# Halved scores in the first half batch, and key pieces placed directly behind score pieces, in a sparse attention and feed-forward kernel

## The chip, the cores and the metric

The kernel runs on one core of one Trainium2 chip. Times are device microseconds (us) of that core for one execution, and a kernel is judged by the median of its runs. Faster and slower mean over 2% away from the kernel before (over 4.67 us here).

## The reference, cut to what matters

```python
# B=4 batches, H=8 heads, S=768 positions, D=64; 8 blocks of 96 positions per head
P = sort_net                                    # [4, 8, 8, 8], five rounds of normalisation
k_sorted = einsum('bhij,bhjcd->bhicd', P, k_b)  # mixes the 8 key blocks of a head
v_sorted = einsum('bhij,bhjcd->bhicd', P, v_b)
attn = softmax(q_block @ k_sorted_block.T / 8)  # within a block: 96 x 96
x = (attn @ v_sorted_block)                     # -> [3072 tokens, 512]
g = s * relu(x @ w_in) ** 2 + b                 # w_in 512 x 2048
out = g @ w_out                                 # w_out 2048 x 512
```

The two large products are nearly all of TensorE's work. Attention is many small matmuls that have to be put between them.

## The kernel before

The program order is written by hand. The 3072 tokens are eight tiles of 384 (two per batch, so tile 2 is the first half of batch 1). `ffn1` computes `hps` (x times w_in) with a "slot" after every pair of 128-row groups; `ffn2` computes `ops` (g times w_out) with a slot after every four matmuls. A queue of small pieces is dealt into the slots.

```python
psa = ctx.enter_context(tc.tile_pool(name="psa", bufs=3, space=PSUM))  # three double banks
psb = ctx.enter_context(tc.tile_pool(name="psb", bufs=2, space=PSUM))  # two single banks

def s_piece(t, hp):                 # scores of two heads: 8 matmuls, then Exp on ScalarE
    sc = psa.tile([BLK, 2, 512], FP, tag="a", name="sc")
    for n in range(HB):
        for e in range(2):
            nc.tensor.matmul(out=sc[:, e, n * BLK:(n + 1) * BLK], lhsT=ks[pr, g0 + n, :], ...)
    nc.scalar.activation(out=at, in_=sc[:, :, 0:TG], func=AF.Exp, scale=scale)

def p_piece(t, hp, n0=0, nn=HB):    # scores times V, then reciprocal and product on VectorE
    ...                             # pv in psb if nn < HB, else in psa
    nc.vector.reciprocal(out=rec[...], in_=pvv[:, :, :, D])
    nc.vector.tensor_tensor(out=x[...], in0=pvv[:, :, :, 0:D], in1=rec[...], op=ALU.mult)

def ffn1(t, slot=nothing, n0=0, nn=HB):
    for f0 in range(0, NF, 2):
        hps = psa.tile([128, 2, 512], FP, tag="a", name="hps")
        ...                         # 8 matmuls
        nc.scalar.activation(out=rt, in_=hps, func=AF.Relu)
        nc.vector.tensor_tensor(out=gt, in0=rt, in1=rt, op=ALU.mult)
        slot()
# k_piece (K): sorted keys "tk" in psa, four casts on VectorE ("v") or ScalarE ("s")
# v_piece1, v_piece2 (V1, V2): sorted values "tv" to DRAM; v_read brings them back as "vs"
# K(2, 32, 16, "s"): batch 2, positions 32 to 63 of each block, casts on ScalarE
# S2(3, 2), P2(3, 2): two s_piece, two p_piece (tile 3, head pairs 2 and 3).  T: x transposed by DMA.  q_turn: q transposed by DMA
gate2: nc.gpsimd.tensor_copy(out=gate2, in_=QT[2][...])   # the read of V waits for q's transpose
v_read(2, nc.gpsimd)
```

`hps`, `sc`, `tk`, `tv` of batches 1 to 3, and a full `pv`, all take turns on three double banks. A piece can start only when the piece three allocations earlier has been evicted.

The softmax here doesn't subtract the row's maximum and nothing guards it: scores larger than these inputs give would overflow.

## Time and profile before

| | before |
|---|---|
| time, median of 3 runs (us) | 233.47 (233.38 to 233.67) |
| span of the profiled run (us) | 231.6 |
| TensorE busy | 97% |
| VectorE, ScalarE busy | about half each |

The prediction shows the busy row, the clock row and the places it starts from. Two more views. The first is the list of what TensorE waited for, above 0.2 us in total (columns: total us, times, longest); it is short, and the first entry and the two cut out come before 17 us, at start-up.

```profile
PE wp L182 <- DVE warm L113: 1.1, 1, 1.1
...
PE ops L516 <- DVE ot L490: 0.4, 1, 0.4
PE hps L473 <- ACT rt L477: 0.3, 1, 0.3
```

The second is TensorE's timeline over the first slots of the first pass (start, duration, operation, count; a bracket gives idle time before it and what ended that). "hps 0" starts at 27.32, "hps 4" at 30.84; no line has a bracket, so nothing waits.

```profile
27.32 1.05 PE L473 MATMUL hps<-xt,wi 128*128 128x192 bf16 x8
28.20 0.30 PE L402 MATMUL pv<-vs,at 96*128 96x66 bf16 x4
28.34 0.83 PE L473 MATMUL hps<-xt,wi 128*128 128x192 bf16 x8
...
30.69 0.31 PE L402 MATMUL pv<-vs,at 96*128 96x66 bf16 x4
30.84 0.83 PE L473 MATMUL hps<-xt,wi 128*128 128x192 bf16 x8
```

### The profile page before, as it was taken

The page shows a single profiled execution, that of the slowest core. Times are in us where ns is not written, and L with a number is a line of the kernel's source. Part 1 is how long each engine was busy: PE and PEld are TensorE (multiplying, and loading weights), DVE is VectorE, ACT ScalarE, POOL GpSimd, SP SyncE. Part 2 cuts the span into 40 slices and gives each one's busy share as a digit, 9 for nine tenths or more (in the row PEclk, how much of TensorE's full clock was granted, in tenths as well). Part 3 has the DMA queues.
Part 4 walks back from the last instruction along what each step waited for, and adds up shares of the span by engine and source line. Part 5 has one row for each costly group of instructions (what it writes and reads, how often), then busy time and mean ns, then how long its engine had stood idle before and what let it go on. Part 6 is the DMA issues. An engine that isn't in the chain of part 4 may idle for free.

```text
span 231.6 us, 4837 instructions
## 1 busy us (share of the span) xinstructions
PE 224.3 (97%) x2036; PEld 136.8 (59%) x2036; DVE 116.8 (50%) x245; ACT 114.6 (49%) x164; POOL 48.3 (21%) x62
## 2 busy tenths in 40 slices
PE   8879999999999999999999999999999999999994
PEld 6779887765544555566555555665555556554442
DVE  5778566638992645244446653343452634432221
ACT  6168479685158486856630645656222236660000
POOL 7820000399992000007920000000000000000000
PEclk9975699999999999999999999999999999999999
DMA  5999999998799992764999995610115240001212
GB/s 93 142 200 211 226 193 205 231 220 183 106 110 180 273 312 63 161 82 65 130 148 133 183 197 115 93 47 0 46 47 113 93 110 4 3 0 45 80 59 91
DMA packets 46695, 28.90 MB, mean 125 GB/s; under 512 B 35921, under 2 KB 41041, under 8 KB 46161
## 3 DMA queue, kind: packets, MB, share of 16 engines
q0 software_dynamic: 18800, 15.21, 47.8%
q1 hardware_dynamic: 27728, 13.32, 26.6%
q8 instruction: 16, 0.26, 0.5%
q10 hardware_dynamic: 144, 0.07, 0.1%
q14 instruction: 7, 0.05, 0.1%
HBM read 29.63 MB, written 8.65 MB: 165 GB/s over the span
## 4 chain that ended last, share of the span: by engine, by line
PE 82%; DVE 7%; DMA 5%; ACT 3%; issue 1%; POOL 0%; POOLq 0%
PE hps L473 35%; PE ops L516 31%; DMA qr<-in_q_dram 5%; PE pv L402 4%; PE sc L375 3%; DVE gt L478 2%; ACT ks L240 2%; DVE ks L238 2%; PE tv L320 2%; PE ops L501 2%; PE tk L294 1%; PE tv L350 1%; PE wp L182 1%; PE tq L254 1%; PE tv L336 1%
## 5 line engine op out<-in xcount | busy, mean ns | idle before, releaser
L473 PE MATMUL hps<-xt,wi 128*128 128x384 bf16 (+1 forms) x576 | 87.1, 309 | 0.3 <-ACT rt L477 0.3
L516 PE MATMUL ops<-wo,gt 128*128 128x512 bf16 x368 | 86.9, 380 | 0.4 <-DVE ot L490 0.4
L473 PEld LDWEIGHTS <-wi 128*128 128x128 bf16 x576 | 54.1, 98 | 30.6 <-issue 1.3
L477 ACT ACTIVATE rt<-hps 128x768 bf16<-128x768 f32 (+1 forms) x72 | 53.1, 741 | 37.4 <-PE hps L473 37.0
L478 DVE TENSOR_TENSOR gt<-rt 128x768 bf16<-128x768 bf16 (+1 forms) x72 | 41.2, 574 | 50.2 <-ACT rt L477 50.0
L516 PEld LDWEIGHTS <-gt 128*128 128x128 bf16 x368 | 33.6, 98 | 37.2 <-issue 1.0
L378 ACT ACTIVATE at<-sc 96x768 bf16<-96x768 f32 x32 | 24.4, 804 | 27.7 <-PE sc L375 27.7
L490 DVE SCALAR_TENSOR_TENSOR ot<-ops,s_bc,bias 128x512 f32<-128x512 f32 x23 | 17.1, 749 | 41.2 <-PE ops L516 41.2
L240 ACT CAST ks<-tk 64x512 bf16<-64x512 f32 (+1 forms) x32 | 18.6, 582 | 10.5 <-PE tk L294 10.2
L407 DVE TENSOR_TENSOR x<-pv,rec 96x512 bf16<-96x512 f32 (+1 forms) x36 | 22.6, 627 | 1.3
L639 POOL TENSOR_TENSOR csum<-csum,wo 128x512 f32<-128x512 f32 x14 | 17.6, 1254 | 1.0
L402 PEld LDWEIGHTS <-at 96*128 96x128 bf16 (+1 forms) x256 | 12.0, 104 | 3.8
L182 PE MATMUL wp<-zt 128*128 128x256 bf16 x86 | 12.9, 311 | 1.1 <-DVE warm L113 1.1
L238 DVE CAST ks<-tk 64x512 bf16<-64x512 f32 (+1 forms) x20 | 13.0, 651 | 1.1 <-PE tk L294 0.8
L402 PE MATMUL pv<-vs,at 96*128 96x66 bf16 (+1 forms) x256 | 13.0, 199 | 0.1
L240 ACT CAST vn<-tv 128x512 bf16<-128x512 f32 (+1 forms) x12 | 9.4, 799 | 7.2 <-PE tv L350 5.0
L375 PEld LDWEIGHTS <-ks 64*96 64x96 bf16 x256 | 8.6, 128 | 5.8 <-issue 5.1
L406 DVE RECIPROCAL rec<-pv 96x8 f32<-96x8 f32 (+1 forms) x36 | 6.9, 192 | 9.5 <-PE pv L402 9.4
L84 POOL DMA_DIRECT2D qr<-in_q_dram x12 | 10.6, 912 | 4.8 <-DMA kb<-in_k_dram 3.1
L375 PE MATMUL sc<-qt,ks 64*96 64x96 bf16 x256 | 10.9, 219 | 0.1
L182 PEld LDWEIGHTS <-zt 128*128 128x128 bf16 x86 | 9.0, 110 | 2.6 <-DVE warm L113 1.1
L294 PEld LDWEIGHTS <-kb 64*128 64x128 bf16 x192 | 6.7, 99 | 3.9 <-issue 3.4
(73 smaller groups left out, 98.4 us busy)
## 6 DMA issues: line engine op xcount, KB each, us to landing
out_dram<-ot SPq DMA_DIRECT2D x23, 256.0 KB, 2.4
kb<-in_k_dram POOLq DMA_DIRECT2D x4, 768.0 KB, 12.2
vb<-in_v_dram POOLq DMA_DIRECT2D x4, 768.0 KB, 19.0
wi<-in_moe_w_in_dram POOLq DMA_DIRECT2D x2, 1024.0 KB, 19.7
wo<-in_moe_w_out_dram POOLq DMA_DIRECT2D x2, 1024.0 KB, 32.6
qr<-in_q_dram POOLq DMA_DIRECT2D x12, 128.0 KB, 13.5
dv<-vn SPq DMA_DIRECT2D x6, 256.0 KB, 7.5
vs<-dv POOLq DMA_DIRECT2D x4, 384.0 KB, 12.7
```

The lines of the kernel that those rows point to most:

```text
L182: nc.tensor.matmul(out=wp, lhsT=zt[:, 0:128], rhs=zt, start=True, stop=True)
L238: nc.vector.tensor_copy(out=out, in_=in_)
L240: nc.scalar.copy(out=out, in_=in_)
L375: nc.tensor.matmul(out=sc[:, e, n * BLK:(n + 1) * BLK], lhsT=ks[pr, g0 + n, :], rhs=QT[b][pr, hp, q0:q0 + BLK], start=True, stop=True)
L378: nc.scalar.activation(out=at, in_=sc[:, :, 0:TG], func=AF.Exp, scale=scale)
L402: nc.tensor.matmul(out=pv[e][0:m, (n - n0) * VW:(n - n0 + 1) * VW], lhsT=atf[:, c0:c0 + m], rhs=VS[b][:, gi, :], start=True, stop=True)
L407: nc.vector.tensor_tensor(out=x[:, n0:n0 + nn, hp * 128:(hp + 1) * 128].rearrange("p n (e d) -> p e n d", e=2), in0=pvv[:, :, :, 0:D], in1 ...
L473: nc.tensor.matmul(out=hps[:, f, 0:nt], lhsT=wi_at(hp, f0 + f), rhs=xt_at(t, hp, n0, nn), start=(hp == 0), stop=(hp == NHP - 1))
L477: nc.scalar.activation(out=rt[:, :, 0:nt], in_=hps[:, :, 0:nt], func=AF.Relu)
L478: nc.vector.tensor_tensor(out=gt[:, f0:f0 + 2, c0:c0 + nt], in0=rt[:, :, 0:nt], in1=rt[:, :, 0:nt], op=ALU.mult)
L516: nc.tensor.matmul(out=ops, lhsT=gt[:, f, m * 128:(m + 1) * 128], rhs=wo_at(f), start=(f == 0), stop=(f == NF - 1))
L639: nc.gpsimd.tensor_tensor(out=csum, in0=csum, in1=wo_at(f), op=ALU.add)
```

## The change

Its intent: in the head, only the half of tile 0's scores that is wanted at once is computed, and the other half is moved into slots of the first pass; one value piece and one score-times-V piece change places; and in batches 2 and 3 a key piece goes directly behind a score piece, so that the drain of TensorE between small and large matmuls is paid once for both.

```diff
+    def s_half(t, hp, n0, nn=2):          # as s_piece, for nn of the four blocks: 4 matmuls
+        sc = psa.tile([BLK, 2, 512], FP, tag="a", name="sc")
...
-    s_piece(0, 0) ... s_piece(0, 3)                    # head, among the value pieces
+    s_half(0, 0, 0) ... s_half(0, 3, 0)
+    def SH(hp):
+        return lambda: (s_half(0, hp, 2), s_half(0, hp + 1, 2))
-    ffn1(0, Queue([P(0, 0, 2, 2), P(0, 1, 2, 2), P(0, 2, 2, 2), P(0, 3, 2, 2),
+    ffn1(0, Queue([SH(0), SH(2), seq(P(0, 0, 2, 2), P(0, 1, 2, 2)),
+                   seq(P(0, 2, 2, 2), P(0, 3, 2, 2)),
                    lambda: q_half(1, "s"), lambda: t_piece(0, "v", 2, 2), SC(1, 0), SC(1, 1)], 8), 0, 2)
-    ... seq(SC(1, 3), P(1, 1)), V1(1), P(1, 2), P(1, 3),
+    ... seq(SC(1, 3), P(1, 1)), P(1, 2), V1(1), P(1, 3),
 # batch 2
-               V2[0], S2(2, 0), V2[1], S2(2, 2), V2[2], V2[3],
+               V2[0], V2[1], S2(2, 0), V2[2], S2(2, 2), V2[3],
-                  seq(T(2), K(2, 0, 16, "s")), P2(3, 0), S2(3, 2), K(2, 32, 16, "s"), P2(3, 2), T(3),
+                  T(2), P2(3, 0), seq(S2(3, 2), K(2, 0, 16, "s")), K(2, 32, 16, "v"), P2(3, 2), T(3),
 # batch 3
-                P2(4, 2), nothing, T(4), K(3, 0, 16, "v"), S2(5, 0), nothing, K(3, 32, 16, "s"),
-                P2(5, 0), nothing, S2(5, 2), nothing, P2(5, 2), K(3, 64, 16, "s"), T(5),
-                lambda: q_turn(3), nothing], 24)
+                P2(4, 2), nothing, T(4), seq(S2(5, 0), K(3, 0, 16, "v")), nothing, nothing, nothing,
+                P2(5, 0), seq(S2(5, 2), K(3, 32, 16, "s")), nothing, nothing, nothing, P2(5, 2),
+                T(5), K(3, 64, 16, "s"), lambda: q_turn(3)], 24)
```

K(2,32) also changes engine, from ScalarE ("s") to VectorE ("v").

More of the change, by code (lines that the diff above doesn't have):

```diff
@@ L379, in s_piece @@
         AT[t, hp] = at
+    def s_half(t, hp, n0, nn=2):
+        b, half = divmod(t, 2)
+        g0 = (b % 2) * 32 + hp * NB + half * HB
+        sc = psa.tile([BLK, 2, 512], FP, tag="a", name="sc")
+        for n in range(n0, n0 + nn):
+            for e in range(2):
+                pr = slice(e * 64, (e + 1) * 64)
+                q0 = (half * HB + n) * BLK
+                nc.tensor.matmul(out=sc[:, e, (n - n0) * BLK:(n - n0 + 1) * BLK],
+                                 lhsT=ks[pr, g0 + n, :], rhs=QT[b][pr, hp, q0:q0 + BLK],
+                                 start=True, stop=True)
+        at = atp.tile([BLK, 2, nn * BLK], BF, tag="at", name="ath")
+        nc.scalar.activation(out=at, in_=sc[:, :, 0:nn * BLK], func=AF.Exp, scale=scale)
+        AT[t, hp, n0] = at
     def p_piece(t, hp, n0=0, nn=HB):
         b, half = divmod(t, 2)
-        at = AT[t, hp]
+        halved = (t, hp, n0) in AT
+        at = AT[t, hp, n0] if halved else AT[t, hp]
         if t not in X:
@@ L398, in p_piece @@
             for n in range(n0, n0 + nn):
-                c0 = (e * HB + n) * BLK
-                m = 128 if c0 + 128 <= 2 * TG else BLK
+                c0 = (e * nn + n - n0) * BLK if halved else (e * HB + n) * BLK
+                m = 128 if c0 + 128 <= at.shape[1] * at.shape[2] else BLK
                 gi = e * 32 + hp * NB + half * HB + n
@@ L594 @@
     v_piece0(32, 16, "v")
-    s_piece(0, 0)
+    s_half(0, 0, 0)
     v_piece0(48, 8, "v")
-    s_piece(0, 1)
+    s_half(0, 1, 0)
     v_piece0(56, 8, "v")
-    s_piece(0, 2)
-    s_piece(0, 3)
+    s_half(0, 2, 0)
+    s_half(0, 3, 0)
     for hp in range(NHP):
@@ L619, in V1 @@
         return lambda: v_piece1(i * 8, eng)
-    ffn1(0, Queue([P(0, 0, 2, 2), P(0, 1, 2, 2), P(0, 2, 2, 2), P(0, 3, 2, 2),
+    def SH(hp):
+        return lambda: (s_half(0, hp, 2), s_half(0, hp + 1, 2))
+    ffn1(0, Queue([SH(0), SH(2), seq(P(0, 0, 2, 2), P(0, 1, 2, 2)),
+                   seq(P(0, 2, 2, 2), P(0, 3, 2, 2)),
                    lambda: q_half(1, "s"), lambda: t_piece(0, "v", 2, 2), SC(1, 0), SC(1, 1)], 8), 0, 2)
-    ffn1(0, Queue([seq(SC(1, 2), P(1, 0)), V1(0), seq(SC(1, 3), P(1, 1)), V1(1), P(1, 2), P(1, 3),
+    ffn1(0, Queue([seq(SC(1, 2), P(1, 0)), V1(0), seq(SC(1, 3), P(1, 1)), P(1, 2), V1(1), P(1, 3),
                    seq(V1(2), V1(3)), lambda: t_piece(1, "v")], 8), 2, 2)
@@ L652 @@
                + [lambda c0=c0: k_piece(1, c0, 16, 1, "vsv"[c0 // 32])() for c0 in range(0, BLK, 32)]
-               + [seq(lambda: load_q(2), lambda: load_k(*brows(2)), bias_piece), V2[0], S2(2, 0), V2[1], S2(2, 2), V2[2], V2[3],
+               + [seq(lambda: load_q(2), lambda: load_k(*brows(2)), bias_piece), V2[0], V2[1], S2(2, 0), V2[2], S2(2, 2), V2[3],
                   P2(2, 0), V2[4], P2(2, 2), V2[5], S2(3, 0),
-                  seq(T(2), K(2, 0, 16, "s")), P2(3, 0), S2(3, 2), K(2, 32, 16, "s"), P2(3, 2), T(3),
+                  T(2), P2(3, 0), seq(S2(3, 2), K(2, 0, 16, "s")), K(2, 32, 16, "v"), P2(3, 2), T(3),
                   seq(lambda: q_turn(2), K(2, 64, 16, "s"))], 24)
```

## The prediction

> **What bounds the kernel now.** I read the page first (busy table, slices, chain), then the chain in order of time, then the timeline of each engine around the four places that the diff touches.
>
> ```profile
> PE 224.3 (97%) x2036; PEld 136.8 (59%) x2036; DVE 116.8 (50%) x245; ACT 114.6 (49%) x164; POOL 48.3 (21%) x62
> PEclk9975699999999999999999999999999999999999
> PE 82%; DVE 7%; DMA 5%; ACT 3%; issue 1%; POOL 0%; POOLq 0%
> ```
>
> TensorE is the bound and hardly ever idle: only work taken off it, or stalls put on it, can move the 233.47 us. The clock row shows the one weak stretch, half clock from 14.1 to 27.8 us (the trace's clock record). The chain shows that VectorE ends the head:
>
> ```profile
> 22.97 0.70 DVE vs L238
> 23.67 0.04 issue
> 23.71 0.38 PE pv L402 x4
> ```
>
> and, from 53.8 to 70.3 us, holds TensorE once more: the bias, then an output eviction, frees a bank at 70.32. Elsewhere the matmuls set the pace. The timeline of TensorE's queue shows what a small piece costs between big matmuls:
>
> ```profile
> 125.90 0.52 PEld L294 LDWEIGHTS <-kb 64*128 64x128 bf16 x16 [0.42 <-issue]
> 127.44 0.43 PEld L375 LDWEIGHTS <-ks 64*96 64x96 bf16 x16 [0.42 <-issue]
> ```
>
> The weight load sits idle before each: it cannot run ahead. By single records, the last ops matmul before a key piece (tk) starts at 125.597 and the piece at 125.908, 0.311 us against the usual 0.216: 0.095 lost going in. The last tk starts at 126.355 and ops at 126.478, 0.123 against 0.029: 0.094 lost coming out. Score pieces (sc) lose 0.093 each way. A round trip costs 0.187 us.
>
> **What the Trainium skill says.** "TensorEngine Tiling (Array Packing)", Key Properties: "Mode switching requires drain". The trace agrees, with the 0.187 us. In the head, 64*96 scores and 64*128 value pieces follow each other without such a gap (score at 22.754 after 22.691, value at 22.666), so a key piece straight behind scores should save one round trip. "TensorE: Matmul & The Clock Gate", What's actually happening: the clock halves or doubles by windows of 3413 ns; the half-clock stretch here is 13.65 us, four such windows. "PSUM — Partial Sum Buffer", PSUM bank collisions: the chip does not arbitrate, so semaphores must keep a writer off a bank being read. The trace agrees: a matmul waits until the eviction of its bank ends (below).
>
> **Part 1, scores in halves.** In the head each score piece drops from 8 to 4 matmuls. At half clock a pair takes 0.09 us, so two pieces ahead of the last value piece free 0.36 us on TensorE. But VectorE still has its two evictions of 0.69 us in a row:
>
> ```profile
> 20.96 1.82 DVE L238 CAST vs<-tv 96x1024 bf16<-96x1024 f32 x2 [0.75 <-PE tv L320]
> 22.97 0.69 DVE L238 CAST vs<-tv 96x512 bf16<-96x512 f32 x1 [0.20 <-PE tv L320]
> ```
>
> The last can start at about 22.70, not 22.97: gain 0.27 us. Followed by half-clock work up to the window's end at 27.77, it is worth only 0.14 us at full clock.
>
> The other halves return in the first pass of hps slots, two pairs of pieces in slots 1 and 2, each with a round trip. There are three double banks for hps, sc and full pv. In the built program (buffers read from its listing) the new score tiles take two of the three, so hps 1 reuses the bank of hps 0 and hps 2 that of hps 1; before, each had its own. ScalarE now sits between:
>
> ```profile
> 28.40 0.49 ACT L477 ACTIVATE rt<-hps 128x384 bf16<-128x384 f32 x1 [1.53 <-PE hps L473]
> ```
>
> With 0.08 us per hps matmul and 0.246 us from last start to end: hps 0's last start 27.98, Relu 28.26 to 28.75; the halves are done by 28.46, so hps 1 waits to 28.79 (0.33). The same again at hps 2: 30.18 (0.33). The pv pieces then come two at a time, and VectorE's program has the third square ahead of them:
>
> ```profile
> 29.20 0.17 DVE L406 RECIPROCAL rec<-pv 96x4 f32<-96x4 f32 x1
> 29.41 0.42 DVE L407 TENSOR_TENSOR x<-pv,rec 96x256 bf16<-96x256 f32 x1
> ```
>
> hps 2's Relu ends 31.53, the square 31.90, the first pair of these 32.46, the second 33.11. The next two pv need exactly these two banks: they want to run at 31.77 and must wait to 32.50 and 33.15 (0.70 and 0.50). hps 4 starts at 33.29; before it started at 30.84. Loss 2.45 us, head gain included: 1.9 of waits, the rest two round trips (0.37) and 0.36 of scores, less the 0.14.
>
> **Part 2, V1 and P swapped.** In the second pass, one hps now waits for a Relu:
>
> ```profile
> 42.99 0.82 PE L473 MATMUL hps<-xt,wi 128*128 128x192 bf16 x8 [0.31 <-ACT rt L477]
> ```
>
> It was ready at 42.51, so 0.48 us is lost. In the new order its bank belongs to the pv two slots earlier, free in time; a new wait of about 0.2 comes for the earlier pv's eviction. Walked through: gain 0.28 us. Front in all: 2.45 - 0.28 = +2.2 us. The VectorE stretch from 54 to 70 starts from these matmuls and moves along.
>
> **Part 3, batch 2.** The order around the bank that comes free at 70.32 puts a value piece (0.43) before it and the score piece (0.49 + 0.093) behind: +0.16. One round trip is saved (-0.19), and so is a 0.14 us wait of S2(3,2) for a key eviction. But the merged key piece takes the bank of the second pv just one slot earlier:
>
> ```profile
> 85.38 0.20 DVE L406 RECIPROCAL rec<-pv 96x8 f32<-96x8 f32 x1 [3.28 <-PE pv L402]
> ...
> 86.52 0.69 DVE L407 TENSOR_TENSOR x<-pv,rec 96x512 bf16<-96x512 f32 x1
> ```
>
> That pv started at 84.91, the bank is free 2.30 us later; the key piece arrives after 0.54 + 0.864 + 0.093 + 0.40 = 1.90: wait 0.4. A pv further on waits 0.14 for the key's four casts (2.36 us on ScalarE). Walked from slot 18 to the first hps: 10.10 us against 9.88, with the 0.16: +0.38.
>
> And the moved key eviction, now on VectorE (four casts, 2.78 us as at 126.68), stands ahead of the last x of tile 3: x ends about 93.4, not 91.7 (+1.7). That feeds a serial queue: transpose of x, six transposes of q, the gate, then the read of V for batch 2.
>
> ```profile
> 91.74 1.28 SPq L452 DMA_TRANSPOSE xt<-x  x1
> 94.49 9.27 SPq L279 DMA_TRANSPOSE qt<-qr  x6
> 105.09 0.18 POOL L663 COPY gate<-qt 1x1 bf16<-1x1 bf16 x1 [34.34 <-DMA qt<-qr]
> ```
>
> That read lands at 116.69 (landing records); the pv that needs it starts at 117.24, so some 0.4 us of slack. 1.7 - 0.38 - 0.4 = a new wait of about 0.9 us there.
>
> **Part 4, batch 3.** Two merged pieces save 0.37. K(3,0) finds its bank free. K(3,32) does not: its pv stands right behind an output eviction on VectorE:
>
> ```profile
> 131.41 0.75 DVE L490 SCALAR_TENSOR_TENSOR ot<-ops,s_bc,bias 128x512 f32<-128x512 f32 x1 [1.95 <-PE ops L516]
> ...
> 133.14 0.69 DVE L407 TENSOR_TENSOR x<-pv,rec 96x512 bf16<-96x512 f32 x1
> ```
>
> The pv starts at 131.22, its second bank is free at 133.83 (+2.61), the key arrives at +1.9 and its scores are held 0.12 too: waits 0.77. Net +0.40.
>
> **Sum.** 2.2 + 0.4 + 0.9 + 0.4 = 3.9, so 233.47 + 3.9 = 237.4; I shade it to 237.0, because every wait is an upper figure when a neighbour is quicker than its row.
>
> **Rivals.** (a) The change does what it means to: fewer scores in the head and three round trips saved, 0.56 + 0.36 + some of the waits, 232.3 us. For it: TensorE is 97% busy and the drains are real. Against it: the bank map, which puts an eviction in front of each merged piece; VectorE, not scores, ends the head. (b) The waits come, but the read of V lands in time (fewer transfers in flight): 236.2. I can't see the transfers' contention. (c) The front's waits leave TensorE idle enough in one 3.41 us window for the clock to halve: up to 1.7 us more, 238.7. The window around 31.2 to 34.6 would be about two thirds busy; the window before 14.1 was some 60% busy with small tiles and fell. I give this 15%. (d) The head's earlier pv lifts the clock one window earlier (24.35, not 27.77): -1.7 us, 235.3. Against it: that window loses scores and gains only 0.27 us of dense work. 5%.
>
> **Range and chances.** The front's +2.2 has some 0.6 either way, the landing 0 to 1.2, batches 2 and 3 some 0.4 each: 235.0 to 238.7. 2% is 4.67 us, 238.14 or 228.80: slower by over 2% needs the clock to fall or every wait to be longer, 18%; faster by over 2% would need a gain four times what the drains can give, 1%.
>
> **What would show it.** Right: hps 4 of the first pass some 2.4 us later, idle before hps 1 and 2 put down to Relu and before the third and fourth pv to VectorE's x; key pieces behind scores with 0.4 and 0.7 us of wait for x and no idle weight load of their own; the first pv of tile 4 waiting for vs<-dv; hps of tile 2 half a microsecond later from the 70.3 anchor. Wrong: those waits absent, hps 4 at the old time, or a gap between scores and key pieces, which would mean the switch is not saved.

## The result, and the profile after

| | before | after |
|---|---|---|
| time, median (us) | 233.47 (233.34 to 233.67, 5 runs) | 237.76 (237.49 to 238.15, 5 runs) |
| ratio | | 1.0185 (95% interval 1.017 to 1.020): slower, but by less than 2% |
| span of the profiled run (us) | 231.6 | 236.3 |

Ratios here and below are the mean time of one kernel's fast runs over that of the other's fast runs of the same rounds, so they are not quite the ratio of the medians quoted. There is a difference: the stretch at half clock near the start lasts three or four of the clock's windows (10.24 or 13.65 us in the traces' clock records), and this varies between runs of one kernel. A run with three has a mean granted clock of 0.975 to 0.978, one with four 0.969 to 0.971. In one set of rounds six runs of the kernel before with three windows read 232.99 to 233.50 and five with four 233.33 to 233.87; their means differ by 0.4 us. Where a difference of that size matters, runs of equal clock are compared.

The page of the changed kernel, the lines that answer to those in the prediction. TensorE is about as busy in microseconds (224.2 against 224.3) in a longer span: the added time is idle time. (20 of its 2036 matmul records are missing from this trace, 2016 are there, so its busy time is up to some 0.8 us too low.) On the chain that ended last, VectorE's share has gone from 7% to 11% and TensorE's from 82% to 76%. The clock row is at 9 from the sixth slice (29.5 us) to the end.

```profile
PE 224.2 (95%) x2016; PEld 137.1 (58%) x2036; DVE 120.4 (51%) x249; ACT 112.4 (48%) x164; POOL 48.2 (20%) x62
PEclk9995699999999999999999999999999999999999
PE 76%; DVE 11%; DMA 4%; ACT 4%; issue 2%; POOL 0%; DVEq 0%
```

What TensorE waited for in the changed kernel. The first three shown are new, and the last has grown from one wait to two; each stands where a step of the prediction put it. Cut out are start-up and the head, a wait behind the bias that was there before (0.6, before 0.4), and 0.8 us put down to "issue", which are five gaps of 0.16 us where a matmul record is missing.

```profile
PE pv L419 <- DMA vs<-dv: 1.2, 1, 1.2
...
PE pv L419 <- DVE x L424: 0.9, 2, 0.6
PE tk L294 <- DVE x L424: 0.9, 2, 0.5
...
PE hps L490 <- ACT rt L494: 0.5, 2, 0.3
```

TensorE's timeline of the same first slots, changed kernel. Hps 1 and hps 2 wait for the Relu of the one before, and then two pv wait for VectorE's x, the product that empties their banks. Hps 4 starts at 33.39 where it started at 30.84.

```profile
27.36 0.94 PE L490 MATMUL hps<-xt,wi 128*128 128x192 bf16 x8
28.23 0.38 PE L390 MATMUL sc<-qt,ks 64*96 64x96 bf16 x8
28.88 0.82 PE L490 MATMUL hps<-xt,wi 128*128 128x192 bf16 x8 [0.27 <-ACT rt L494]
...
30.28 0.82 PE L490 MATMUL hps<-xt,wi 128*128 128x192 bf16 x8 [0.27 <-ACT rt L494]
...
32.62 0.31 PE L419 MATMUL pv<-vs,ath 96*128 96x66 bf16 x4 [0.58 <-DVE x L424]
33.25 0.30 PE L419 MATMUL pv<-vs,ath 96*128 96x66 bf16 x4 [0.32 <-DVE x L424]
33.39 0.83 PE L490 MATMUL hps<-xt,wi 128*128 128x192 bf16 x8
```

The bracket counts idle time after the modelled end of the matmul before, so it understates the delay. I therefore also compare the gap from the last start of one piece to the first start of the next, by single records, with the same gap where nothing waits. Hps 1 comes 0.475 us after scores instead of 0.138: a wait of 0.34, and the same at hps 2. The third pv comes 0.827 us after hps instead of 0.083: 0.74; the fourth 0.50 later than a pair would. Together 1.92 us.

The timelines further on, changed kernel: the merged key pieces and the first pv of tile 4. K(2,0) and K(3,32) wait for x, K(3,0) does not, and the pv waits for the read of V.

```profile
88.44 0.56 PE L375 MATMUL sc<-qt,ks 64*96 64x96 bf16 x16
89.39 0.62 PE L294 MATMUL tk<-pd,kb 64*128 64x64 bf16 x16 [0.40 <-DVE x L424]
...
121.59 0.58 PE L419 MATMUL pv<-vs,at 96*128 96x66 bf16 x13 [1.17 <-DMA vs<-dv]
...
130.65 0.63 PE L294 MATMUL tk<-pd,kb 64*128 64x64 bf16 x16
...
137.35 0.64 PE L294 MATMUL tk<-pd,kb 64*128 64x64 bf16 x16 [0.46 <-DVE x L424]
```

Start to start, K(3,0) follows its scores by 0.044 us, where a key piece behind large matmuls takes 0.311: the saved drain is real. K(2,0) takes 0.600, K(3,32) 0.665.

The way to the late read of V, in the timelines of VectorE, of SyncE's DMA queue and of GpSimd, changed kernel: the key casts run from 91.59, x of tile 3 ends at 96.18 (before: 91.68), its transpose starts at 96.25 (before: 91.74), and the gate is passed at 109.10 (before: 105.09).

```profile
91.59 2.79 DVE L238 CAST ks<-tk 64x512 bf16<-64x512 f32 x4 [1.69 <-PE tk L294]
...
95.49 0.69 DVE L424 TENSOR_TENSOR x<-pv,rec 96x512 bf16<-96x512 f32 x1
```

```profile
96.25 1.28 SPq L469 DMA_TRANSPOSE xt<-x  x1
...
99.00 8.82 SPq L279 DMA_TRANSPOSE qt<-qr  x6
```

```profile
109.10 0.18 POOL L684 COPY gate<-qt 1x1 bf16<-1x1 bf16 x1 [35.80 <-DMA qt<-qr]
```

The starts of six common points in the two profiled runs show where the 4.7 us of span came in:

| first start of | before | after | later by | so this stretch added |
|---|---|---|---|---|
| hps 4, first pass | 30.84 | 33.39 | 2.55 | 2.55 |
| hps of tile 1 | 47.08 | 49.59 | 2.51 | -0.04 |
| ops behind the bias | 70.32 | 72.87 | 2.55 | 0.04 |
| hps of tile 2 (batch 2's slots done) | 92.38 | 95.40 | 3.02 | 0.47 |
| first pv of tile 4 | 117.24 | 121.59 | 4.35 | 1.33 |
| hps of tile 4 (batch 3's slots done) | 140.47 | 145.19 | 4.73 | 0.37 |

### The profile page after: what moved, and what is told of

It is laid out like the page before. It is cut to its first block, busy times and chain, and to the rows that moved or that the text cites. A ratio compares the mean times of both kernels' runs of the same rounds, so it can differ in the third digit from the quotient of the medians.

```text
span 236.3 us, 4822 instructions
## 1 busy us (share of the span) xinstructions
PE 224.2 (95%) x2016; PEld 137.1 (58%) x2036; DVE 120.4 (51%) x249; ACT 112.4 (48%) x164; POOL 48.2 (20%) x62
## 4 chain that ended last, share of the span: by engine, by line
PE 76%; DVE 11%; DMA 4%; ACT 4%; issue 2%; POOL 0%; DVEq 0%
PE hps L490 30%; PE ops L533 29%; PE wp L182 6%; DMA vs<-dv 4%; PE pv L419 3%; DVE gt L495 3%; PE sc L375 2%; DVE x L424 2%; DVE ks L238 2%; ACT rt L494 2%; PE ops L518 1%; PE tk L294 1%; PE tv L320 1%; ACT ks L240 1%; DVE vs L238 1%
## 5 line engine op out<-in xcount | busy, mean ns | idle before, releaser
L533 PE MATMUL ops<-wo,gt 128*128 128x512 bf16 x349 | 83.1, 379 | 2.2 <-issue 0.8
L378 ACT ACTIVATE at<-sc 96x768 bf16<-96x768 f32 x28 | 21.3, 803 | 32.3 <-PE sc L375 32.3
L240 ACT CAST ks<-tk 64x512 bf16<-64x512 f32 (+1 forms) x28 | 16.3, 583 | 11.9 <-PE tk L294 11.6
L238 DVE CAST ks<-tk 64x512 bf16<-64x512 f32 (+1 forms) x24 | 15.9, 661 | 2.9 <-PE tk L294 2.6
L182 PE MATMUL wp<-zt 128*128 128x256 bf16 x86 | 14.2, 334 | 1.1 <-DVE warm L113 1.1
L419 PEld LDWEIGHTS <-at 96*128 96x128 bf16 x224 | 9.6, 102 | 4.4 <-issue 1.6
L182 PEld LDWEIGHTS <-zt 128*128 128x128 bf16 x86 | 9.8, 120 | 3.3 <-DVE warm L113 1.1
L419 PE MATMUL pv<-vs,at 96*128 96x66 bf16 x224 | 10.1, 195 | 1.2 <-DMA vs<-dv 1.2
L375 PEld LDWEIGHTS <-ks 64*96 64x96 bf16 x224 | 6.3, 121 | 5.8 <-issue 5.1
L375 PE MATMUL sc<-qt,ks 64*96 64x96 bf16 x224 | 8.4, 210 | 0.0
```

Source lines behind the costliest of these rows:

```text
L182: nc.tensor.matmul(out=wp, lhsT=zt[:, 0:128], rhs=zt, start=True, stop=True)
L238: nc.vector.tensor_copy(out=out, in_=in_)
L240: nc.scalar.copy(out=out, in_=in_)
L419: nc.tensor.matmul(out=pv[e][0:m, (n - n0) * VW:(n - n0 + 1) * VW], lhsT=atf[:, c0:c0 + m], rhs=VS[b][:, gi, :], start=True, stop=True)
L533: nc.tensor.matmul(out=ops, lhsT=gt[:, f, m * 128:(m + 1) * 128], rhs=wo_at(f), start=(f == 0), stop=(f == NF - 1))
```

## The experiments

The theory from here on is the prediction's own: most moves put a bank's next user too close behind its last one, so that evictions on ScalarE and VectorE, and one read of V behind them, set the pace. Its rivals: the added pieces cost their TensorE time as such, or the clock does it. Eleven kernels were run besides the two, all with correct results; they are labelled e1 to e11. "Before" in each paragraph is the kernel before in the same rounds.

**The halved scores alone.** (e1) The kernel before with the head and the first pass of the change, nothing else.

> The kernel before with the halved scores alone (head and the first four hps slots as in the change; nothing else). My account (waits for Relu and for the x evictions): 2.3 to 2.5 us slower, 235.9 us; the fifth hps group of the first pass starts 2.4 us later than before after the same start of the value pieces, with idle TensorE before hps 1 and 2 (0.27 each, Relu) and before the third and fourth pv (0.6 and 0.3, x). Rival, the loss is only the added work (two round trips 0.37 and 0.36 of scores, head gain off): 0.5 to 0.8 us slower, 234.1 us, and the rest of the 4.3 us lies in the key pieces.

```diff
-    s_piece(0, hp) in the head;  P(0, 0, 2, 2), P(0, 1, 2, 2), P(0, 2, 2, 2), P(0, 3, 2, 2)
+    s_half(0, hp, 0) in the head;  SH(0), SH(2), two P per slot
```

236.36 us (235.97 to 236.47, 4 runs) against 233.35; ratio 1.0125 (1.0111 to 1.0139), a loss of 3.0 us. All four runs had the fourth half-clock window, so hps 0 and the first halves ran at half clock; against runs of before with four windows the loss is about 2.6 us. In its profile hps 4 starts at 33.89, 3.05 us after its old place where 2.4 was expected; but its half clock lasted to 29.12 and that of before to 27.77, so runs with equally many windows are still not quite alike. The profile's list of waits has the two of the theory, with the sizes they have in the changed kernel:

```profile
PE pv L419 <- DVE x L424: 0.9, 2, 0.6
PE hps L490 <- ACT rt L494: 0.6, 2, 0.3
```

**The swap alone.** (e2) `V1(1), P(1, 2)` becomes `P(1, 2), V1(1)`.

> The kernel before with only the pv piece and the value piece of batch 1 swapped in the second pass. By the prediction 0.28 us faster (a 0.48 us wait for Relu replaced by 0.2 for an x eviction), 233.2 us. By the trace of the changed kernel, where the hps groups gained 0.16 and then waited 0.12 for the transposed x, nearly nothing: 0 to 0.1 us.

```diff
-    seq(SC(1, 3), P(1, 1)), V1(1), P(1, 2), P(1, 3),
+    seq(SC(1, 3), P(1, 1)), P(1, 2), V1(1), P(1, 3),
```

233.28 us (233.11 to 233.68) against 233.35; ratio 0.9997 (0.9985 to 1.001). In the times it is worth nothing that can be measured, not the predicted 0.28 us. The traces resolve a little: from hps 4 to hps of tile 1 it takes 16.20 us, against 16.24 before.

**The two queues of batches 2 and 3 alone.** (e3)

> The kernel before with only the two queues of batches 2 and 3 as in the change (key pieces moved, value pieces reordered). My account: 0.47 (batch 2) + 1.33 (the first pv of tile 4 waits for the read of V) + 0.37 (batch 3) = 2.2 us slower, 235.6 us, and with the halves alone the two sum to the whole 4.3 to 4.7. Rival, the late read of V comes from the front's delay and not from the key eviction: no such wait here, 0.8 us slower, 234.3 us.

```diff
 # the batch 2 and batch 3 parts of the change, on the kernel before
```

235.38 us (235.0 to 235.73) against 233.35; ratio 1.0085 (1.007 to 1.0101), 2.0 us. The wait for the read of V is there without the front's part, so it comes from the queue of batch 2:

```profile
PE pv L419 <- DMA vs<-dv: 1.0, 1, 1.0
```

The two parts run alone lose 2.6 us (at equal clock) and 2.0 us; their sum 4.6 is close to the change's 4.3 in the medians and 4.7 in the profiled runs.

**The second key piece evicted by ScalarE again.** (e4) The changed kernel, one letter different, so that the key casts are no longer ahead of x on VectorE.

> The changed kernel with one letter different: the second key piece of batch 2 is evicted by ScalarE instead of VectorE. My account: x of tile 3 ends 1.4 us earlier, so the transposes of q, the gate and the read of V start 1.4 us earlier, and the 1.33 us wait of the first pv of tile 4 goes: 1.2 to 1.4 us faster than the changed kernel, 236.4 us. Rival, the read is late because of other transfers beside it: wait and time as in the changed kernel, 237.7 us.

```diff
-    K(2, 32, 16, "v"), P2(3, 2), T(3),
+    K(2, 32, 16, "s"), P2(3, 2), T(3),
```

237.0 us (236.38 to 237.17, 4 runs); ratio to before 1.015 (1.0134 to 1.0167). At equal clock it is 1.1 to 1.4 us faster than the changed kernel, and the wait for `vs<-dv` is gone from the list. It is gone only just: by the landing records the read is complete at 119.83, and the pv starts at 119.97.

**The other order on VectorE.** (e9) A second test of the same chain, by another means: the casts stay on VectorE, but P2(3,2) and so the last x go first.

> The changed kernel with one exchange in batch 2: the scores-times-V piece P2(3,2) goes ahead of the second key piece K(2,32), whose eviction stays on VectorE. My theory: the V read of batch 2 is late because the four key casts stand ahead of the last x of tile 3 on VectorE. Then x of tile 3 ends some 2 us earlier, the wait of the first pv of tile 4 for vs<-dv (1.2 us) is gone, and the time falls by 1.1 to 1.4 us from the changed kernel: ratio to before 1.012 to 1.014. Rival (the read is late because ScalarE's or the matmuls' share moved, or because the transfers collide): the wait for vs<-dv stays at 0.8 us or more and the ratio stays at 1.017 to 1.020.

```diff
-    K(2, 32, 16, "v"), P2(3, 2), T(3),
+    P2(3, 2), K(2, 32, 16, "v"), T(3),
```

236.77 us (236.43 to 237.04, 4 runs) against 233.47; ratio 1.0141 (1.0122 to 1.0159), at the upper edge of what was expected and clear of the rival's 1.017. X of tile 3 is transposed from 93.60 instead of 96.25, the read is complete at 119.09, and the pv follows the matmuls before it without a bracket:

```profile
118.69 2.11 PE L533 MATMUL ops<-wo,gt 128*128 128x512 bf16 x9
120.63 0.70 PE L419 MATMUL pv<-vs,at 96*128 96x66 bf16 x16
```

From hps of tile 2 to this pv it takes 24.86 us, against 26.19 in the changed kernel: 1.33 us, the whole wait. Moving the eviction to the other engine and moving it behind x have the same effect, so the order of VectorE's queue is the cause.

**Batch 3's queue alone, and the same with one piece moved.** In the first (e5), batch 3 is as in the change. In the second (e6), P2(5,0) goes one slot earlier, so that its banks are free when K(3,32) arrives.

> The kernel before with only the queue of batch 3 as in the change. My account: two mode switches saved (0.37) and 0.77 of waits for x at the second merged key piece: 0.37 to 0.4 us slower from the first ops of that queue to the first hps after it (27.27 us before), total 0.2% slower. Rival, the merging saves what it means to: 0.37 us faster there.

> The same queue, but the pv pieces of the second half stand one slot earlier, so that two slots lie between them and the scores with the second key piece, and no output eviction stands before them on VectorE. My account: both waits go and the two saved switches stay: the queue takes 0.37 us less than in the kernel before, total 233.0 us. Rival, the drain is not saved by standing behind scores: no less than before.

```diff
-    seq(S2(5, 0), K(3, 0, 16, "v")), nothing, nothing, nothing, P2(5, 0), seq(S2(5, 2), K(3, 32, 16, "s")),
+    seq(S2(5, 0), K(3, 0, 16, "v")), nothing, nothing, P2(5, 0), nothing, seq(S2(5, 2), K(3, 32, 16, "s")),
```

As in the change: 233.69 us (233.49 to 234.23) against 233.56, ratio 1.0012 (0.9998 to 1.0026). From hps of tile 2 to that of tile 4 it takes 48.46 us against 48.08 before, +0.38, which the profile resolves and the times don't. With the piece moved: 232.81 us (232.70 to 233.37), ratio 0.9972 (0.9959 to 0.9985), the same stretch 47.66, -0.42. The timeline of K(3,32) in each, first as in the change, then moved:

```profile
131.67 0.72 PE L375 MATMUL sc<-qt,ks 64*96 64x96 bf16 x16
132.85 0.64 PE L294 MATMUL tk<-pd,kb 64*128 64x64 bf16 x16 [0.46 <-DVE x L424]
```

```profile
131.77 0.56 PE L375 MATMUL sc<-qt,ks 64*96 64x96 bf16 x16
132.17 0.63 PE L294 MATMUL tk<-pd,kb 64*128 64x64 bf16 x16
```

So a merged piece does save its drain (two save 0.42 us), and in the change the wait for a bank took more than it gave. One slot decides the sign.

**A first attempt at a better kernel.** (e7) The swap, batch 3 moved as above, and in batch 2 K(2,0) behind S2(3,0) with its eviction on VectorE. The load of K for batch 2 is also issued before that of q.

> A candidate to beat both: whole scores in the head, the swap of the second pass, the queue of batch 3 with the pv pieces one slot earlier, and in batch 2 the first key piece straight behind the scores of tile 3's first half (evicted by VectorE; K loaded before q so that it is there). Where three switches are saved and no bank is in use: 0.37 + 0.19 + 0.14 (a wait of scores for a key eviction) + 0.1 = 0.8 us faster than the kernel before, 232.6 us at equal clock. It fails to reach that if the earlier key eviction delays the x of the next pv, or the read of V.

```diff
-    seq(lambda: load_q(2), lambda: load_k(*brows(2)), bias_piece)
+    seq(lambda: load_k(*brows(2)), lambda: load_q(2), bias_piece)
-    V2[5], S2(3, 0), seq(T(2), K(2, 0, 16, "s")), P2(3, 0), S2(3, 2), K(2, 32, 16, "s"), ...
+    V2[5], seq(S2(3, 0), K(2, 0, 16, "v")), T(2), P2(3, 0), S2(3, 2), K(2, 32, 16, "s"), ...
```

233.63 us (232.97 to 234.0) against 233.56; ratio 0.9999 (0.9983 to 1.0014): a miss. Two things went against it. Five of its six runs had the fourth half-clock window, against seven of eleven of before; at equal clock it is 0.1 us faster with four windows, and 0.4 with three (one run). And in batch 2 the casts on VectorE delayed the x behind them, so the second half of S2(3,2) waited:

```profile
86.76 0.38 PE L375 MATMUL sc<-qt,ks 64*96 64x96 bf16 x8
87.51 0.38 PE L375 MATMUL sc<-qt,ks 64*96 64x96 bf16 x8 [0.37 <-DVE x L424]
```

From the ops behind the bias to hps of tile 2 it took 22.28 us against 22.06 before, +0.22. It is the same mistake as the change's: a key eviction on VectorE in front of an x.

**The same with the eviction left on ScalarE** (e10), without the swap.

> The kernel before with batch 3 of e6 (P2(5,0) one slot early) and, in batch 2, only the first key piece moved behind the score piece S2(3,0), its eviction left on ScalarE. If a merged piece is worth its saved round trip wherever its bank is free, this gains 0.19 us on e6: ratio 0.996 (0.9945 to 0.9975), 232.6 us at equal clock windows, with 0.04 us between the last score and the first key matmul in batch 2 and no wait for x above 0.2 us at S2(3,2). Rival: the earlier key eviction delays a later bank as in e7, S2(3,2) or P2(3,0) waits 0.3 us or more, and the ratio is 0.997 to 0.999, no better than e6.

```diff
-    V2[5], S2(3, 0), seq(T(2), K(2, 0, 16, "s")), P2(3, 0),
+    V2[5], seq(S2(3, 0), K(2, 0, 16, "s")), T(2), P2(3, 0),
```

232.67 us (232.43 to 232.93, 5 runs) against 233.47; ratio 0.997 (0.9957 to 0.9983). In the profile batch 2's stretch takes 21.87 us against 22.06, the 0.19 us of one drain. It does not come as I wrote: the key piece follows its scores by 0.20 us, not 0.04, so part of the saving is lost there. No bank causes this: the trace shows the key piece released by the read of K, which landed at 82.41 where the scores' last matmul started at 82.26. In e7, whose K was loaded first and landed at 75.97, the key piece followed its scores by 0.042. As much is won back where S2(3,2) no longer waits for a key eviction (gap 0.309 instead of 0.450 before). In the times it can't be told from the kernel with batch 3 alone (0.9972), whose rounds were others. It is faster than both kernels of this study, in the medians by 0.8 us against the kernel before (0.6 to 0.8 at equal clock): real, and far under 2%.

**The halves, one per slot.** (e8) If the four waits are most of the front's loss, the same halves spread out should cost little more than their drains.

> The halves alone as in e1_halves, but the returning halves come one to a slot and the pv pieces one to a slot, so that no bank is taken back within two slots and none of the waits for Relu and x should be left. Work stays, with two round trips more than in e1_halves. My account: the waits are 1.9 of the 2.4 us, so this is 0.9 to 1.2 us slower than the kernel before, 234.4 us, against some 3.0 of e1_halves. Rival, the loss is the added work: as slow as e1_halves or slower, as there are more switches.

```diff
-    ffn1(0, Queue([SH(0), SH(2), seq(P(0, 0, 2, 2), P(0, 1, 2, 2)), seq(P(0, 2, 2, 2), P(0, 3, 2, 2)),
-                   q_half, t_piece, SC(1, 0), SC(1, 1)], 8), 0, 2)
+    ffn1(0, Queue([HF(0), HF(1), seq(HF(2), P(0, 0, 2, 2)), seq(HF(3), P(0, 1, 2, 2)),
+                   seq(P(0, 2, 2, 2), q_half), P(0, 3, 2, 2), seq(t_piece, SC(1, 0)), SC(1, 1)], 8), 0, 2)
```

236.38 us (235.79 to 236.61) against 233.56; ratio 1.0113 (1.0098 to 1.0129): a miss. The four waits are gone, but my order made a fifth, seen in the timelines of TensorE, ScalarE and VectorE:

```profile
36.56 0.26 PE L447 MATMUL tr<-ident,x 96*128 96x96 bf16 x2 [1.11 <-DVE x L424]
```

```profile
33.67 1.50 ACT L240 COPY qt<-tq 128x768 bf16<-128x768 bf16 x2 [0.53 <-PE tq L254]
35.06 0.89 ACT L494 ACTIVATE rt<-hps 128x384 bf16<-128x384 f32 x2
```

```profile
35.60 0.36 DVE L495 TENSOR_TENSOR gt<-rt 128x384 bf16<-128x384 bf16 x1 [1.52 <-ACT rt L494]
35.88 0.17 DVE L423 RECIPROCAL rec<-pv 96x4 f32<-96x4 f32 x1
36.08 0.42 DVE L424 TENSOR_TENSOR x<-pv,rec 96x256 bf16<-96x256 f32 x1
```

Read it backwards: the transposes wait for the last x, x stands on VectorE behind a square (gt), the square waits for its Relu, and the Relu stands on ScalarE behind 1.50 us of q copies that I had put one slot too early. The transposes were held up by three queues in turn.

**The halves, one per slot, with q behind the last pv.** (e11)

> The kernel before with the halved scores, but the returned halves one per slot, each pv piece one per slot behind the next half, the query piece behind the last pv, so that no Relu, square or q cast stands in front of a bank wanted next (what I had missed in e8). Theory (four waits are most of the +2.5 us): hps 4 of the first pass comes 0.5 to 1.0 us after its old place (30.84), no wait above 0.3 us for Relu or x and none of 1 us at the transposes; time 233.47 + 0.4 to 0.9, ratio 1.002 to 1.005 at the same number of half-clock windows. Rival (halves cost their time as such, or the clock does it): ratio 1.009 or more again with no wait named.

```diff
+    ffn1(0, Queue([HF(0), seq(HF(1), P(0, 0, 2, 2)), seq(HF(2), P(0, 1, 2, 2)), seq(HF(3), P(0, 2, 2, 2)),
+                   P(0, 3, 2, 2), q_half, seq(t_piece, SC(1, 0)), SC(1, 1)], 8), 0, 2)
```

235.44 us (234.76 to 235.66, 6 runs) against 233.47; ratio 1.0086 (1.0071 to 1.01). The first half of the expectation holds, the second does not. Hps 4 starts at 31.74, 0.90 us after its old place, and no line before it has a bracket:

```profile
28.14 0.29 PE L390 MATMUL sc<-qt,ks 64*96 64x96 bf16 x4
28.36 0.83 PE L490 MATMUL hps<-xt,wi 128*128 128x192 bf16 x8
29.13 0.29 PE L390 MATMUL sc<-qt,ks 64*96 64x96 bf16 x4
29.35 0.31 PE L419 MATMUL pv<-vs,ath 96*128 96x66 bf16 x4
...
31.74 0.83 PE L490 MATMUL hps<-xt,wi 128*128 128x192 bf16 x8
```

That is about what four separate halves should cost: four drains of 0.187 and 0.36 us of scores are 1.1 us, against 1.04 measured from hps 0 to hps 4 beyond before, where this order has one pv piece less (the fourth comes behind hps 4). By the first hps of tile 1 it is 1.45 us later than before (48.53 against 47.08). The 0.55 us more are that pv piece and two waits of 0.24 and 0.20 us at later hps: one for the q copies on ScalarE, and one for the copy of the transposed x, which stands on VectorE behind a square whose Relu stands behind the q copies. The time is 2.0 us worse in the medians, 1.5 to 1.8 at equal clock. The ratio lies where the rival put it, at 1.009, but with waits that can be named. For the change this means: 1.9 of its front's 2.5 us are the four waits, which another order does without, but that order paid for two more drains and for waits further on. I found no order in which the halves pay.

## Why the prediction was right

237.0 us was predicted and 237.76 measured, inside the range and on the right side of zero, and the mechanism was right in its main parts: new waits for evicted banks and for a read, nearly all put down by the profile to the engines that the prediction had named. Two terms were mis-sized: the swap, and the wait for the read of V. The sizes, step by step:

- **Halved scores, +2.45.** Measured +2.55 at hps 4. The four waits, 0.33, 0.33, 0.70 and 0.50, came as 0.34, 0.34, 0.74 and 0.50. The halves alone give nearly the same waits, the spread order (e11) has none of them and hps 4 moves to +0.90. The two profiled runs differ in clock (half clock to 27.77 before, to 27.29 after) and in when the value pieces start (17.95 and 18.15), which nearly cancels: from that start to hps 4, five three-window traces with the old front (e2, e3, e5, e6, e10) take 12.62 to 12.74 us, and the two with the new one (the changed kernel and e4) 15.24 and 15.20, so at equal clock the loss is about 2.5 too.
- **The head's gain.** The last eviction was to move from 22.97 to 22.70. It did become the third of three in a row on VectorE, but the value pieces began 0.20 us later in the profiled run (18.15 against 17.95), so the first pv came at 23.70 instead of 23.71. The kept traces show the gain apart from that: from the start of the value pieces to the first pv it takes 5.73 to 5.77 us in the seven kernels with whole scores in the head and 5.55 to 5.57 in the six with halves. It is 0.2 us, at half clock.
- **The swap, -0.28.** Wrong in size. In the changed kernel the hps behind it gains 0.16 us (2.55 late before, 2.38 late after): the new wait for the earlier pv's eviction took 0.31, not 0.2. The first hps of tile 1 then waits 0.12 longer, for the transposed x, so 0.04 is left; alone, the swap is worth the same 0.04 in the traces and nothing in the times. The step that failed is "walked through: gain 0.28 us": the walk stopped before the transposes of tile 1, whose eviction ends the pass.
- **Batch 2, +0.38.** Measured +0.47. The wait of K(2,0) for x was to be 0.4; it is 0.40 by the bracket, which understates, and 0.56 by the gap (0.600 against 0.044). The pv further on, which was to wait 0.14, did not wait (its gap is the usual 0.216). New is a wait of 0.09 of hps of tile 2 for an x that stood behind the key casts on VectorE; without those casts there (e4) the stretch takes 0.39 longer than before.
- **The read of V, +0.9.** Measured +1.33, the largest error in the sum. The chain was right and two experiments confirm it. (The profile's own chain puts the read's first issue down to a Relu on ScalarE; but that issue starts 0.73 to 0.75 us after the gate does in all thirteen traces, so it is the gate that sets it.) Its terms: the gate was to be 1.3 us later than hps of tile 2 and was 1.0 (4.01 less 3.02; q's six transposes took 8.82 us, not 9.27). The slack was 0.4 in the trace of before. But the second transfer of the read, the one this pv waits for, took 10.25 us from issue to landing instead of 9.51 (landing records: 107.19 to 116.70 before, 111.20 to 121.46 after), +0.75. 1.0 - 0.4 + 0.75 is about the 1.33. The prediction had kept the transfer's length and called contention something it could not see. That length is not the change's doing as far as the runs show: over all thirteen traces it goes from 9.44 to 10.48, and in the six other kernels with batch 2's queue as before it is 10.13, 10.48, 10.40, 9.87, 10.34 and 9.44, without a wait. The slack in these six goes from 0.04 to 1.4. So the 0.9 rested on one trace's slack and transfer; what makes the transfer vary is open.
- **Batch 3, +0.40.** Measured +0.37, and alone +0.38. The wait of 0.77 came as 0.62 at the key piece and 0.17 within its scores. (The terms shown in the working, 2.61 less 1.9 and 0.12, do not give 0.77 exactly.) The saved drains were to give 0.37; with the wait removed the stretch gained 0.42.
- **The shading.** The working summed to 3.9 and I took 3.5, "because every wait is an upper figure when a neighbour is quicker than its row". The medians differ by 4.3: the waits were not upper figures.

The rivals: (a), the intended gain, fails at every merged piece but K(3,0). (b), V in time, is what the kernel with the eviction back on ScalarE shows, at 237.0 (236.38 in its run with three windows), and not what the change does. (c), a second fall of the clock, did not happen: the clock row is at 9 from 29.5 us on, through the window where it was to fall. (d), a window fewer, does happen in some runs of either kernel and is not an effect of the change that these runs could show: 16 of the 31 runs of the kernel before in the experiments' rounds had three windows, and 10 of the 28 runs of the six kernels with halved scores. The Trainium skill, "TensorE: Matmul & The Clock Gate", What's actually happening, says that the window is free-running and the number of cold matmuls varies from run to run; these runs agree, with three or four windows in the same kernel. I had read four windows in one profile as the kernel's property.

## What to carry to other kernels

Before putting a piece directly behind another to save a drain, write down whose bank it takes, when that bank's eviction ends and when its own input lands; a saving of 0.19 us is lost to a wait of 0.6 to 0.8 if the two are one slot too close, and moving the earlier piece one slot turns the sign. When an eviction changes engine, list what stands behind it on the new engine's queue and follow that to the next transfer: here four casts on VectorE led to a wait of 1.3 us two stages and 30 us later. A move that leaves TensorE's work the same but fills two slots and empties two others is to be judged by the waits at both, and the walk must go on to the next point that both orders share.

## What the Trainium skill lacked or had wrong

- "TensorEngine Tiling (Array Packing)", Key Properties, says that changing the tiling mode drains TensorE but gives no cost. Here a small piece between large matmuls loses 0.187 us in and out, and 64*128 keys directly behind 64*96 scores lose none of it (0.044 us start to start, against 0.311 behind 128*128 matmuls).
- "TensorE: Matmul & The Clock Gate", What's actually happening, warns that the cold stretch varies and advises not to fit to it. It does not say that runs have to be sorted by it when small effects are measured: three or four half-clock windows made about 0.4 us here, as much as each part of the change in batches 2 and 3 apart from the read of V.
- "PSUM — Partial Sum Buffer", PSUM bank collisions raise a hardware error, gives the rule that a bank must be guarded, and no measure of what the guard costs when a bank is taken up again too soon: 0.34 us behind a Relu of 0.49 us, 0.50 to 0.74 us behind a reciprocal and a product of together 0.6 us with a square ahead of them.
- None of these three pages bears on the read of V, and I looked up no page for it: 9.44 to 10.48 us from issue to landing for the same bytes in thirteen traces, a spread of 1.0 us that the runs leave unexplained.
